# Output steps of a fused attention, GLU and MLP kernel: sums in SBUF or in the output's DRAM rows

## The chip, the core and the metric

The kernel runs on one core of one Trainium2 chip. The metric is the device time of one execution in microseconds (us), here the median of three runs.

## The reference, cut to what matters

Three layers follow one another on 2304 tokens (4 sequences of 576) with a model width of 512. The first is a linear attention over 8 heads, the second a gated MLP (GLU) with d_ff 1536, the third an MLP with d_ff 2048. The change concerns the last product of the third:

```python
def _moe2_ref(x, w_in, w_out) -> np.ndarray:
    h = x @ w_in
    g = h * (1.0 / (1.0 + np.exp(-h)))
    return (g @ w_out).astype(np.float32)
```

The weights are float64 in DRAM. Inputs and outputs of the matmuls are float32, and each operand is split into a high and a low part, so that a product is three matmuls (high x high, high x low, low x high; the list `PASS`).

## The kernel before, in words

Tokens stand in 18 tiles of 128 rows, in five blocks: blocks 0 to 3 of 512 tokens, block 4 of 256. The d_ff of the two MLPs is walked in groups (`groups`). A group of the third layer holds two slices of 128 columns, `fs`, so there are eight groups, from 575.85 us of the span to its end. All 18 tiles pass through each group, so every output element is a sum over eight groups, which is kept in SBUF, in the tiles `ya` (called `o` in `g2_mlp`).

A group does three things. It makes h = SiLU(x @ w_in) for each slice and block: matmuls into a PSUM buffer g (L205; for blocks 0 and 1 the sharing scheme of `quad`, L539; block 4 uses a y buffer), SiLU on ScalarE (ACT, L239 or L562), the high half of h on ACT (L198) and the low half on VectorE (DVE, L199). It makes the output steps (`g2_mlp`, L279): per tile six matmuls into one of four PSUM buffers y (L292), then in the first group a copy to SBUF on ACT (L301), in the seven later groups an add of PSUM to SBUF on DVE (L303). In the last group each finished tile is stored from SyncE's queue (SP, L306); the last tile is done in two halves of 256 columns there. The two tiles of block 4 have rows in two sequences, so that each is stored by two transfers (`out_rows`, L62).

And a group prepares the weights of the next one. SP loads 512 KB of float64 words (L134, L136). DVE shifts and masks them in five operations of 128x512 (L146 to L157), GpSimd (Pool) finishes the float32 value with two integer adds (L160), ACT rounds the high part (L412) and DVE subtracts to get the low part (L416). For the sharing scheme Pool also makes four small sums of the two w_in slices (`sum12`, `sum34`, through `less`, L319), which go through L412 and L416, too.

The order of the work is the order in which the program emits it, and each engine's queue keeps it: the generator `stream` yields after pieces of matmul work, and `WeightQueue.tick` is called at a pace to put the next piece of weight preparation between them. In groups 3 to 7 (the third to the seventh) the emission runs: decode of both w_in slices (`dec`, whose last two steps are L160 on Pool); third-layer matmuls of slice 0 for block 2; step 1 of block 1; high part of the first weight; step 2; its low part and the high part of the second weight; steps 3 and 4; low part, `sum12`; SiLU of slice 0 for block 2; `sum34`; slice 1 for block 2; step 1 of block 0; high part of the first sum; steps 2 to 4; high part of the second sum and decode of the first w_out slice; SiLU of slice 1 for block 2; slice 0 for block 3 with its SiLU; step 1 of block 2; high part of that w_out slice and decode of the second; the other steps of block 2; slice 1 for block 3, both slices for block 4. The steps of blocks 3 and 4 are emitted between the products of the next group's `quad`.

Of the kernel before, what the change touches and what calls it, by code (L numbers as in the profile page):

```python
# [13 lines left out]
AF = mybir.ActivationFunctionType  # L14
ALU = mybir.AluOpType
# [5 lines left out]
def kernel(  # L21
# [14 lines left out]
    nc = tc.nc  # L36
# [8 lines left out]
    TB = 4  # L45
# [16 lines left out]
    def out_rows(i):  # L62
        kind, b, hf, r = tiles[i]
        if kind == "m":
            r0 = b * S + 256 * hf
            return [(0, P, out[r0:r0 + 256, :].rearrange("(p r) d -> p r d", r=2)[:, r, :])]
        return [
            (64 * e, 64 * e + 64, out[(b + e) * S + 512:(b + e) * S + 576, :]) for e in range(2)
        ]
# [29 lines left out]
    def ps_tile(which, shape):  # L99
        p, tag, n = pools[which]  # L100
        return p.tile(shape, F32, tag=tag, name=tag, bufs=n)
# [177 lines left out]
    def g2_mlp(fs, j, hs, first, last, end):  # L279
        wq.need(*[(2, "p", f) for f in fs])  # L280
        nt = blocks[j] // P
        o = ya[j].rearrange("p (t d) -> p t d", t=nt)
        nn = 3 * len(fs)
        cuts = [(t, 0, DM) for t in range(nt)]
        if end:
            cuts[-1:] = [(nt - 1, d, d + DM // 2) for d in (0, DM // 2)]
        for t, d0, d1 in cuts:
            ps = ps_tile("ps_y", [P, DM])[:, d0:d1]
            n = 0
            for f in fs:  # L290
                for a, c in PASS:
                    nc.tensor.matmul(  # L292
                        out=ps,
                        lhsT=hs[f][:, a, t * P:(t + 1) * P],
                        rhs=wt[2, "p", f][:, c, d0:d1],
                        start=(n == 0),
                        stop=(n == nn - 1),
                    )
                    n += 1
            if first:  # L300
                nc.scalar.activation(out=o[:, t, :], in_=ps, func=AF.Copy)  # L301
            else:
                nc.vector.tensor_tensor(out=o[:, t, d0:d1], in0=ps, in1=o[:, t, d0:d1], op=ALU.add)  # L303
            if last:
                for p0, p1, rows in out_rows(j * TB + t):
                    nc.sync.dma_start(out=rows[:, d0:d1], in_=o[p0:p1, t, d0:d1])  # L306
            yield 0.216 * nn

    KH = KC // 2
# [368 lines left out]
    def stream():  # L678
# [25 lines left out]
        for u, (kind, fs) in enumerate(groups):  # L704
# [4 lines left out]
            if std <= u < std + NSTD:  # L709
                out_of = lambda j: g2_mlp(fs, j, hs[j], first, False, False)  # L710
                ys = iter(pend)
                wq.hold = first
                while wait:
                    wait.pop(0)()
                each = [(2, 1), (2, 2), (1, 0), (2, 1)] if first else [(2, 2), (1, 1), (0, 0), (0, 0)]
                for n, k in enumerate(each):
                    if n == 3:
                        ys = chain_of(ys, out_of(0))
                        wq.release(*wq.keys(u - 1)[1])
                    yield from mlp_block(fs[n % 2], n // 2, hs[n // 2], ys, k if n < 3 else (k[0], 9))  # L720
                wq.hold = False
                if first:
                    assert wq.jobs.pop(0)[0] == 1 << 10
                    now, later = token_sums(
                        lambda k: w_tile(1, 7, F32) if k == 2 else wq.slot(("t", k), F32),
                        lambda n: wq.release(("t", 1 - n)),
                    )
                    sums.extend(now)
                if u == std + NSTD - 1:
                    sums.extend(later)  # L730
                yield from g1_mlp(fs[0], 2, hs[2], (), out_of(1))
                yield from g1_mlp(fs[1], 2, hs[2], (), ())
            else:
                yield from quad(u, iter(pend), hs)
# [6 lines left out]
            if kind == 1:  # L741
                f = fs[0]
                out_of = lambda j: g2_glu(fs, j, hs[j], False, done)
                ys = chain_of(out_of(0), out_of(1))
                yield from glu_block(f, 2, hs[2], ys, {"g": 0, "v": 1})
                yield from glu_block(f, 3, hs[3], ys, {"g": 1, "v": 1})
                yield from glu_block(f, 4, hs[4], ys, {"g": 1, "v": 1})
                yield from ys
                pend = chain_of(out_of(2), out_of(3), out_of(4))
                wq.release(*wq.keys(u)[0])  # L750
            else:
                out_of = lambda j, end=False: g2_mlp(fs, j, hs[j], first, last, end)
                if u >= std + NSTD:
                    for n, f in enumerate(fs):
                        yield from g1_mlp(f, 2, hs[2], (), out_of(1 - n))
                if last:
                    yield from g1_mlp(fs[0], 4, hs[4], (), ())
                    yield from g1_mlp(fs[1], 4, hs[4], (), out_of(2))
                    yield from g1_mlp(fs[0], 3, hs[3], (), ())
                    yield from g1_mlp(fs[1], 3, hs[3], out_of(4), ())  # L760
                    yield from out_of(3, True)
                else:
                    yield from g1_mlp(fs[0], 3, hs[3], out_of(2), ())
                    yield from g1_mlp(fs[1], 3, hs[3], (), ())
                    for f in fs:
                        yield from g1_mlp(f, 4, hs[4], (), ())
                    wq.release(*wq.keys(u)[0])
                    pend = chain_of(out_of(3), out_of(4))
# [697 lines left out]
    with tc.manual_schedule():  # L1466
# [21 lines left out]
        def idle(n, deps):  # L1488
            o = Op("warm", "PE", 0.21 * n, warm(n), deps, ["b"])
            o.free.append((o, "b"))  # L1490
            return o
# [4 lines left out]
                out=om, in_=omega.rearrange("m (o d) -> m o d", o=1).to_broadcast([P, 2, D])  # L1496
# [3 lines left out]
        first = idle(5, [])  # L1500
# [74 lines left out]
```

## Time and profile before

| | us |
|---|---|
| median of 3 runs (954.39 to 955.02) | 954.68 |
| the profiled execution, its own time | 954.74 |
| span of the profiled execution, first to last instruction | 952.9 |
| TensorE busy in the span | 942.4 |
| VectorE busy | 705.6 |
| ScalarE busy | 431.9 |
| GpSimd busy | 414.0 |

Busy times count an instruction from its start to its end; issuing DMAs and waiting on semaphores is not counted. PE is TensorE, DVE VectorE, ACT ScalarE, POOL GpSimd, SP SyncE; SPq is the queue of DMA issues on SP. L303 is line 303 of the kernel before. `out<-in` gives the tiles by the program's names: `ya` the sums in SBUF, `y` and `g` PSUM buffers, `m` and `raw` weights in work, `w` and `ws` finished weights and their sums, `h` and `s` activations. A time line has one row for a run of like instructions: start, length, engine, line, and in brackets how long the engine had waited and for whom. In a row by windows the numbers behind the length are the busy times of PE, PEld, DVE, ACT and POOL, each with its count of instructions, then the granted clock of TensorE (1.00 is the full level, 2.4 GHz), the mean share of the 16 DMA engines and GB/s.

### The profile page before, as it was taken

The numbers are of one execution on the slowest core, as the hardware profiler recorded it, in microseconds if no ns is written. First come the engines' busy times: TensorE is split into PE (matmuls) and PEld (weight loads), VectorE is DVE, ScalarE is ACT, GpSimd is POOL, SyncE is SP. The second block draws the span as 40 slices with busy tenths as digits, with TensorE's granted clock in tenths as the row PEclk, the third lists the DMA queues.
The fourth block names the chain that finished last, engine by engine and source line by source line (L and its number), as shares of the span: only waits on it lengthen the run. The fifth ranks groups of instructions, "written<-read, shape, count | busy, mean of one in ns | idle before, by whom it ended". The sixth has DMA issues, their size and how long they took to land.

```text
span 952.9 us, 17029 instructions
## 1 busy us (share of the span) xinstructions
PE 942.4 (99%) x6570; PEld 791.5 (83%) x6570; DVE 705.6 (74%) x1368; ACT 431.9 (45%) x978; POOL 414.0 (43%) x402
## 2 busy tenths in 40 slices
PE   8999999999999999999999999999999999999998
PEld 6888878888888888888888887878888888888887
DVE  6998989648687878779778785887757676767543
ACT  6999977543424323433333355543333333333321
POOL 8888655315445445436335204552424242424200
PEclk9999999999999999999999999999999999999999
DMA  7645443002111121021112100211111111111023
GB/s 181 176 124 157 136 126 101 12 23 74 58 46 45 45 67 45 23 66 52 38 45 67 45 1 27 63 44 45 45 45 45 45 45 45 44 45 45 1 78 122
DMA packets 79489, 60.42 MB, mean 63 GB/s; under 512 B 27312, under 2 KB 73648, under 8 KB 79408
## 3 DMA queue, kind: packets, MB, share of 16 engines
q1 hardware_dynamic: 79136, 59.26, 21.4%
q8 instruction: 52, 0.85, 0.4%
q14 instruction: 29, 0.24, 0.1%
q10 hardware_dynamic: 272, 0.07, 0.0%
HBM read 49.87 MB, written 4.72 MB: 57 GB/s over the span
## 4 chain that ended last, share of the span: by engine, by line
PE 93%; DVE 3%; ACT 1%; DMA 1%; POOL 1%; SPq 1%; issue 0%; DVEq 0%
PE g L205 23%; PE y L292 20%; PE g L539 15%; PE y L259 13%; PE y L205 6%; PE b L1043 3%; PE b L205 2%; PE b L1443 2%; PE kv L1123 2%; PE b L1227 2%; PE b L1016 2%; PE b L1203 1%; PE b L1323 1%; DVE h L199 1%; SPq L1183 0%
## 5 line engine op out<-in xcount | busy, mean ns | idle before, releaser
L160 POOL TENSOR_TENSOR m<-m,raw 128x512 int32<-128x512 int32 x136 | 202.5, 1491 | 322.3 <-issue 209.2
L205 PE MATMUL g<-xs,w 128*128 128x512 f32 x1056 | 256.1, 389 | 0.0
L205 PEld LDWEIGHTS g<-xs,w 128*128 128x128 f32 x1056 | 197.5, 188 | 40.5
L292 PE MATMUL y<-w,h 128*128 128x512 f32 (+1 forms) x870 | 206.9, 388 | 2.3 <-DVE ya L270 1.6
L292 PEld LDWEIGHTS y<-w,h 128*128 128x128 f32 x870 | 162.4, 188 | 36.4 <-issue 1.8
L199 DVE TENSOR_TENSOR h<-s,h 128x512 fp32r<-128x512 f32 (+1 forms) x134 | 107.8, 809 | 77.5 <-ACT h L198 76.4
L259 PE MATMUL y<-h,w 128*128 128x512 f32 (+1 forms) x648 | 155.4, 366 | 0.0
L270 DVE TENSOR_TENSOR ya<-y,ya 128x512 f32<-128x512 f32 (+1 forms) x200 | 122.8, 631 | 20.9 <-PE y L259 20.7
L259 PEld LDWEIGHTS y<-h,w 128*128 128x128 f32 x648 | 113.2, 188 | 20.4 <-DVE h L199 0.5
L303 DVE TENSOR_TENSOR ya<-y,ya 128x512 f32<-128x512 f32 (+1 forms) x127 | 84.4, 680 | 54.4 <-PE y L292 53.9
L198 ACT ACTIVATE h<-s 128x512 fp32r<-128x512 f32 (+1 forms) x134 | 77.1, 585 | 93.7 <-DVE s L644 49.4
L539 PE MATMUL g<-xs,w 128*128 128x512 f32 x360 | 91.7, 390 | 0.0
L412 ACT ACTIVATE w<-m 128x512 fp32r<-128x512 f32 x74 | 46.6, 629 | 84.0 <-POOL m L160 77.4
L416 DVE TENSOR_TENSOR w<-m,w 128x512 fp32r<-128x512 f32 x65 | 66.5, 1024 | 22.2 <-ACT w L412 21.1
L1092 ACT ACTIVATE e<-b,nb 128x128 f32<-128x128 f32 x272 | 75.8, 422 | 7.6 <-PE b L205 2.8
L539 PEld LDWEIGHTS g<-xs,w 128*128 128x128 f32 x360 | 67.1, 188 | 13.9
L539 PE MATMUL g<-w,w 128*128 128x512 f32 x270 | 68.7, 390 | 0.0
L205 PEld LDWEIGHTS y<-xs,w 128*128 128x128 f32 x480 | 60.6, 188 | 2.3
L205 PE MATMUL y<-xs,w 128*128 128x256 f32 x480 | 61.3, 280 | 0.0
L539 PEld LDWEIGHTS g<-w,w 128*128 128x128 f32 x270 | 50.1, 188 | 10.0
L1060 DVE TENSOR_REDUCE small<-b 128x4 f32<-128x512 f32 (+1 forms) x80 | 51.4, 643 | 6.9 <-PE b L1043 3.2
L562 ACT ACTIVATE s<-s 128x512 f32<-128x512 f32 x21 | 13.3, 632 | 77.7 <-DVE s L567 77.7
(120 smaller groups left out, 1159.8 us busy)
## 6 DMA issues: line engine op xcount, KB each, us to landing
raw<-in_moe_w_out_dram SPq DMA_DIRECT2D x28, 512.0 KB, 3.5
raw<-in_moe_w_in_dram SPq DMA_DIRECT2D x16, 512.0 KB, 3.7
raw<-in_moe_w_gate_dram SPq DMA_DIRECT2D x12, 512.0 KB, 3.6
raw<-in_moe_w_val_dram SPq DMA_DIRECT2D x12, 512.0 KB, 3.6
qT<-e SPq DMA_DIRECT2D x72, 64.0 KB, 2.5
x<-in_k_dram SPq DMA_DIRECT2D x16, 256.0 KB, 3.8
x<-in_q_dram SPq DMA_DIRECT2D x16, 256.0 KB, 3.4
va<-in_v_dram SPq DMA_DIRECT2D x32, 128.0 KB, 4.2
```

The lines of the kernel that those rows point to most:

```text
L160: tt(out=mi, in0=mi, in1=(low if step == 5 else high).bitcast(I32), op=ALU.add)
L198: nc.scalar.activation(out=ht[:, 0, :], in_=s, func=AF.Copy)
L199: nc.vector.tensor_tensor(out=ht[:, 1, :], in0=s, in1=ht[:, 0, :].bitcast(F32), op=ALU.subtract)
L205: nc.tensor.matmul(out=ps, lhsT=w[:, a, cc * P:(cc + 1) * P], rhs=xs[j][:, c, cc, :], start=(n == 0), stop=(n == 3 * KC - 1),)
L259: nc.tensor.matmul(out=ps, lhsT=wt[1, "o", f][:, a, d * P:(d + 1) * P], rhs=hs[f][:, c, :], start=(n == 0), stop=(n == nn - 1),)
L270: nc.vector.tensor_tensor(out=y[:, d, :], in0=ps, in1=y[:, d, :], op=ALU.add)
L292: nc.tensor.matmul(out=ps, lhsT=hs[f][:, a, t * P:(t + 1) * P], rhs=wt[2, "p", f][:, c, d0:d1], start=(n == 0), stop=(n == nn - 1),)
L303: nc.vector.tensor_tensor(out=o[:, t, d0:d1], in0=ps, in1=o[:, t, d0:d1], op=ALU.add)
L416: eng.tensor_tensor(out=v[:, 1, :], in0=x, in1=v[:, 0, :].bitcast(F32), op=ALU.subtract)
L539: nc.tensor.matmul(out=ps, lhsT=w[:, a, (c0 + c) * P:(c0 + c + 1) * P], rhs=x(b, c), start=(start and n == 0), stop=(n == 3 * KH - 1), ski ...
L1060: nc.vector.tensor_reduce(out=st.mx.rearrange("p (j e) -> p e j", e=2)[:, e], in_=st.ps[e], axis=AX.X, op=ALU.max)
L1092: nc.scalar.activation(out=st.e[r][:, :, h, :] if blocks4 else st.e[r][:, h, :], in_=src.rearrange("p (a f) -> p a f", a=4) if blocks4 els ...
```

## The change

Every output step is copied from PSUM to its place in SBUF by ACT, whichever group it is in. Right after that a transfer takes it to the output's rows in DRAM: in the first group a plain store from SP's queue, in the later seven a transfer from GpSimd's queue that adds to what stands in the rows. The adds on DVE and the stores of the last group fall away. A group has 18 steps and 20 transfers (two for each tile of block 4); with the halved last tile there are 20 plain stores and 141 adding transfers.

```diff
--- before.py
+++ after.py
@@ -297,13 +297,12 @@
                         stop=(n == nn - 1),
                     )
                     n += 1
-            if first:
-                nc.scalar.activation(out=o[:, t, :], in_=ps, func=AF.Copy)
-            else:
-                nc.vector.tensor_tensor(out=o[:, t, d0:d1], in0=ps, in1=o[:, t, d0:d1], op=ALU.add)
-            if last:
-                for p0, p1, rows in out_rows(j * TB + t):
+            nc.scalar.activation(out=o[:, t, d0:d1], in_=ps, func=AF.Copy)
+            for p0, p1, rows in out_rows(j * TB + t):
+                if first:
                     nc.sync.dma_start(out=rows[:, d0:d1], in_=o[p0:p1, t, d0:d1])
+                else:
+                    nc.gpsimd.dma_start(out=rows[:, d0:d1], in_=o[p0:p1, t, d0:d1], accum_op=ALU.add)
             yield 0.216 * nn
 
     KH = KC // 2
```

## Rows read from the trace of the kernel before

**Rows 1.** The page's parts 1 and 4: engines' busy time, chain that ended last.

```profile
PE 942.4 (99%) x6570; PEld 791.5 (83%) x6570; DVE 705.6 (74%) x1368; ACT 431.9 (45%) x978; POOL 414.0 (43%) x402
...
PE 93%; DVE 3%; ACT 1%; DMA 1%; POOL 1%; SPq 1%; issue 0%; DVEq 0%
```

**Rows 2.** Windows: stretch, length, busy time of the engines, clock, DMA share, GB/s.

```profile
622.00:652.03 30.03, 29.34 (x131) 23.91 (x130) 26.39 (x41) 9.33 (x15) 15.48 (x11) 1.00 0.12 35
702.60:750.35 47.75, 47.75 (x224) 40.01 (x223) 32.55 (x56) 16.52 (x29) 16.83 (x12) 1.00 0.13 40
893.59:949.62 56.03, 56.02 (x265) 46.86 (x263) 24.30 (x38) 14.37 (x26) 0.00 (x0) 1.00 0.22 75
575.85:949.62 373.77, 373.06 (x1741) 312.26 (x1740) 247.62 (x407) 134.17 (x236) 126.84 (x84) 1.00 0.15 48
```

**Rows 3.** The chain in order of time, 622 to 640 us: start, length, what.

```profile
627.65 1.19 DVE ya L303 x2
...
631.83 1.20 DVE ya L303 x2
633.03 0.75 DVE h L199
```

**Rows 4.** Waits of one group, 702.6 to 750.35: in all, times, longest.

```profile
ACT w L412 <- POOL m L160: 11.0, 3, 6.8
...
ACT w L412 <- POOL m L319: 1.2, 1, 1.2
```

**Rows 5.** Groups of instructions, 702.6 to 750.35; the last row from 576 to 952.9.

```profile
L160 POOL TENSOR_TENSOR m<-m,raw 128x512 int32<-128x512 int32 x8 | 13.2, 1650 | 31.4 <-DVE m L157 24.3 <-issue 6.7
L303 DVE TENSOR_TENSOR ya<-y,ya 128x512 f32<-128x512 f32 x18 | 12.0, 683 | 7.0 <-PE y L292 7.0
...
L149 DVE TENSOR_SCALAR raw<-raw 128x512 uint32<-128x512 uint32 x4 | 1.7, 420 | 0.0
...
L319 POOL TENSOR_TENSOR ws<-ws,m 128x256 f32<-128x256 f32 x1 | 1.1, 1090 | 0.1
...
L301 ACT ACTIVATE ya<-y 128x512 f32<-128x512 f32 x18 | 10.7, 597 | 15.3 <-PE y L292 15.2
```

**Rows 6.** The chain in order of time in the same group: start, length, what.

```profile
731.20 5.44 PE y L292 x24
736.64 2.72 PE g L205 x12
739.36 5.44 PE y L292 x24
```

**Rows 7.** Time line of Pool, same group: start, length, what, wait before.

```profile
724.53 7.08 POOL L160 TENSOR_TENSOR m<-m,raw 128x512 int32<-128x512 int32 x4 [24.35 <-DVE m L157]
731.69 0.74 POOL L319 TENSOR_TENSOR ws<-m 128x256 f32<-128x256 f32 x1
...
734.71 0.73 POOL L319 TENSOR_TENSOR m<-m,ws 128x256 f32<-128x256 f32 x1
```

**Rows 8.** Time line of ACT in the same group.

```profile
731.64 0.63 ACT L412 ACTIVATE w<-m 128x512 fp32r<-128x512 f32 x1 [2.35 <-POOL m L160]
...
735.48 0.63 ACT L412 ACTIVATE w<-m 128x512 fp32r<-128x512 f32 x1 [1.22 <-POOL m L319]
736.02 0.58 ACT L239 ACTIVATE s<-g 128x512 f32<-128x512 f32 x1
736.63 0.63 ACT L198 ACTIVATE h<-s 128x512 fp32r<-128x512 f32 x1
```

**Rows 9.** Time line of the end, all engines.

```profile
941.21 8.39 PE L292 MATMUL y<-w,h 128*128 128x512 f32 x42
...
942.04 0.63 ACT L198 ACTIVATE h<-s 128x512 fp32r<-128x512 f32 x1
...
949.64 0.42 DVE L303 TENSOR_TENSOR ya<-y,ya 128x256 f32<-128x256 f32 x1 [0.29 <-PE y L292]
```

**Rows 10.** Loads on the page; the final store's issue and landing; SP's waits, 570 to 952.9.

```profile
raw<-in_moe_w_in_dram SPq DMA_DIRECT2D x16, 512.0 KB, 3.7
...
L306 SPq DMA_DIRECT2D out_dram<-ya x21: 332/333/1127, 916.1 to 950.1; - x21
...
DMA to landing us min/median/max: 1.8/2.1/3.0
...
SPq L306 <- DVE ya L303: 64.8, 16, 40.9
```

## The prediction

> **What bounds the kernel now.** I read the page first. Its span is 952.9 us and TensorE (PE) is busy for 942.4 us of it [rows 1]; the chain that ended last is 93% PE. Only code after 575.85 us changes, so I cut that stage with the view by windows [rows 2]: from 575.85 to 949.62 us PE is busy 373.06 of 373.77 us at the full granted clock. That is 0.71 us of idle time, nearly all of it (30.03 - 29.34) in one place, 622 to 652 us, where PE waits for DVE's low half of h [rows 3]. So nothing can be won in this stage beyond 0.71 us. The question is only what new waits the change makes.
>
> The stage repeats every 47.75 us, one group of two d_ff slices over all five blocks: 18 output steps of six matmuls. In such a group DVE is busy 32.55 us, ACT 16.52 and Pool 16.83 [rows 2]: room on average. But each engine works in program order, and the list of waits [rows 4] shows ACT standing behind Pool for 11.0 us (the weights' high halves, L412, wait for the integer adds of L160). I therefore follow one group in the chain in order of time, which is PE here, and in the time lines of Pool and ACT [rows 6 to 8].
>
> **The change, part by part.**
>
> *Removed.* 127 DVE adds: 18 of 683 ns in a group, 12.0 us [rows 5]. DVE does not bound PE except in the one stall above, on whose chain two pairs of these adds stand [rows 3]. Gain: at most the 0.71 us; I take 0.7. The 21 final stores leave SP, too.
>
> *Added on ACT.* The same steps copied at 597 ns, as the 18 first-group copies show [rows 5]: 10.7 us a group, ACT then 27.2 of 47.75 us. Each copy must free one of four y buffers, and some now stand behind ACT's waits for Pool. Where L412 waits until 731.64 [rows 8], the copies of the third and fourth step of the stretch at 723 us end at about 732.9 and 733.5; PE takes their buffers again at 733.9 and 735.3 (731.20 plus two and three steps of 1.36, [rows 6]). Price nothing, with 1 us of slack.
>
> *First group.* Its 20 plain stores (18 steps, two of them in two halves) go into SP's queue ahead of weight loads: 20 x 0.333 = 6.7 us of issue [rows 10], each waiting for its ACT copy. Behind them wait the raw loads, and for those DVE's decode; a load takes 3.7 us [rows 10] and stands most of a group ahead of its use. I price it at nothing; without that lead it would delay a decode by a step, 1.4 us.
>
> *Added on Pool.* The adding transfers: 20 a group. Let d be Pool's time for issuing one. No row shows it. From below: an SP issue takes 0.33 us [rows 10]. From above: the longest Pool instruction of the group, the L160 add at 1.65 us on average [rows 5]; past 1.55 Pool itself is full (second rival), so this forecast's own range ends there. I take d = 1.1, as the small Pool add of 1.09 us [rows 5] is the nearest thing of Pool's own that is mostly handling. The Trainium skill ("DMA: Bandwidth & Descriptors", Specifications) gives GpSimd's path about 1 us to the first byte and SP's 0.6; by it, as an estimate, the sum below would come to about 971. No run here shows that yet.
>
> Each transfer waits for its ACT copy, and Pool's adds queue behind. Program order on Pool becomes: four L160 adds, transfers 1 to 4, the four sum adds (L319), transfers 5 to 8, two L160 adds, and so on. Today the L160 adds end at 731.61 and the sums follow at once until 735.44 [rows 7]; ACT's last sum copy starts at 735.48, the SiLU that follows at 736.02, its h copy at 736.63 [rows 8]. That h is needed by the output step that starts at 739.36 [rows 6]: its low half at the sixth matmul, about 740.5, so the high half must be ready, with DVE's 0.7, by 739.8. Today it is ready at 737.26 (736.63 + 0.63): slack 2.5 us.
>
> With the change the sums start later by S, the larger of 4d (four issues in a row) and 1.95 + d (the fourth copy ends about 0.63 + 2 x 0.6 us after the adds, with 0.1 for the handing over). For d = 1.1, S = 4.4. Added to it: 0.6 because the decode begins after one more ACT copy and 0.4 for copies crowding between the sum copies. Stall of PE per group: 4.4 + 0.6 + 0.4 - 2.5 = **2.9 us**. Bounds: d = 0.33 gives S = 2.3, a stall of 0.8; d = 1.55 gives S = 6.2, a stall of 4.7. Later in the group, the same reckoning leaves PE unhindered: the weights' second pair is used a group later.
>
> Five groups have this pattern; the group at 622 to 652 us has it in another order, with half the transfers ahead of the sums, and I take half, 1.5 us (0 to 3). Sum: 5 x 2.9 + 1.5 = 16.0.
>
> *The transfers themselves.* 18 x 256 KB = 4.7 MB a group. The last window moved 75 GB/s at a DMA share of 0.22 [rows 2], about 2.9 us of all engines per MB. Taken as read and write at twice that, the transfers need 27 of 47.75 us beside the 0.13 of today: hidden. They would bind at over three times the plain price. That a transfer waits for the one before it I exclude: the stores of before go to one output too, several in flight, and SP's waits have only the adds [rows 10]. The row's earlier transfer is a group old.
>
> *The tail.* Today PE ends at 949.62, the half add takes 0.42, SP issues at once and the store lands 2.1 us later [rows 9, 10]. With the change the last seven copies feed nine transfers, the first copy ending at 943.4, behind ACT's h at 942.67 [rows 9]: at d = 1.1 Pool ends the ninth issue at 943.4 + 9.9 = 953.3, against SP's 950.4: +2.9. One pass through the output rows more: 0 to 2.1, I take 1.0. Tail +3.9; at d = 0.33 it is +0.1 to +2, at d = 1.55 about +8.
>
> **Sum.** The profiled execution took 954.74 us, against a median of 954.68. 954.74 - 0.7 + 16.0 + 3.9 = **973.9**. With the bounds of d: 954.74 - 0.7 + 4 + 0.5 + 1 = 959.5, and 954.74 - 0.7 + 23.5 + 2.5 + 8 = 988.
>
> **Rivals.**
> 1. *Hidden (15%).* The slack of 2.5 us is enough, since DVE is freer and Pool's L160 adds shorten (two-input DVE work beside them falls by 12 us a group), and d is near 0.33. Only the tail grows: 954.74 - 0.7 + 1 to 4 = 955 to 959. For it: low mean load of ACT and Pool. Against: Pool's order, whatever d is, since the fourth copy alone holds the sums back by 1.85 us.
> 2. *Pool, or the DMA engines, become the bound (20%).* Point of decision: 20 d + 16.83 > 47.75, d > 1.55. At d = 2 the group takes 56.8, 9.1 us more, six times, and the tail 12: 954.74 - 0.7 + 54.6 + 12 = 1021. Accumulating at over three times the plain transfer price has the same effect. DVE's decode runs 20 shift and mask operations of 0.42 us a group [rows 5]; if Pool could issue nothing beside them, 8.4 us more would lie on Pool and the point of decision would fall to d = 1.13, close to what I take. That is why this rival has as much as 20%. The Trainium skill ("SBUF — State Buffer", Who interferes with whom) speaks for this: by it, a DVE operation in a two-port mode holds the port that GpSimd needs to write its transfers' descriptors. The rows only hint at it: the L160 adds take 1.65 us on average in this group.
> 3. *Each transfer waits for the former (4%).* 20 x (2.1 + d) + 16.83 = 81 us a group: +33 x 6, about 1155. Against it [rows 10].
> 4. *Not slower (3%).* The DVE chain at 622 to 640 us [rows 3] loses its 2.4 us of adds and PE its stall; the tail stays, because the transfers' issue is no longer than SP's 0.33. Then 954.74 - 0.7 = 954.0. It decides where S stays under 2.5 - 1.0 us, so that every h keeps its slack.
>
> **How the numbers follow.** The forecast gets 58%, its own range 959.5 to 988. The range of 8 in 10 reaches from 957 (half of rival 1) to 1008 (half of rival 2). About 0.2%, 1.9 us, is what a measurement of this kernel can tell from no change. Faster by more would need 1.9 us where PE idles only 0.71: 1%. Same: rival 4 and a third of rival 1, 7%. Slower: 92%.
>
> **What would show it.** DVE's L303 gone, ACT copies of about 0.6 us, Pool instructions or gaps of about 1.1 us per transfer. PE idle of 2 to 4 us once a group, at the output steps after the third g product, released by DVE's or ACT's h (L199, L198); ACT's wait at L412 for Pool's L319 sums grown from about 1 to over 4 us. Wrong: PE as full as before (rival 1), Pool without gaps and the stall elsewhere (rival 2), Pool waiting on DMA (rival 3), or stalls caused by y buffers that ACT frees late.

## The result, and the profile after

| | before | after |
|---|---|---|
| median, us | 954.77 (4 runs, 954.39 to 955.02) | 967.16 (4 runs, 966.57 to 970.18) |
| the profiled execution, its own time | 954.74 | 967.20 |
| its span | 952.9 | 965.4 |

The ratio is 1.0136, with a 95% interval of 1.0115 to 1.0158: 12.4 us slower. The prediction was slower, 973.9 us, so its direction held, the measured time lies inside both of its ranges, and the forecast loss of 19.2 us was too large by 6.8.

The page of after, its parts 1 and 4 and a row of its DMA issues (KB each, median us to landing), beside [rows 1]:

```profile
PE 945.7 (98%) x6570; PEld 790.7 (82%) x6570; DVE 643.2 (67%) x1241; ACT 499.4 (52%) x1105; POOL 533.0 (55%) x543
...
PE 75%; POOL 8%; ACT 7%; DVE 5%; issue 2%; DMA 2%; SPq 1%; POOLq 0%; DVEq 0%; ACTq 0%
...
out_dram<-ya POOLq DMA_DIRECT2D x111, 256.0 KB, 6.1
```

127 DVE instructions are gone, ACT has 127 more, and Pool has 141 more, the adding transfers, which the page counts as busy. On average no engine came nearer to full than PE. But PE's share of the chain that ended last fell from 93% to 75%. A part of that lies ahead of the stage (ACT's L1091, 2%); within it, Pool and ACT now end waits of PE, as the rows below show.

Where the 12.5 us of span went is read from the chain of waits in order of time. Each group of the last six begins with a product of the sharing scheme (L539, in after L538, 549 and the like). The starts of three of them in after, at 704.52, 753.27 and 803.37, against 702.60, 750.35 and 798.10 before:

```profile
704.52 1.39 PE g L538 x6
...
753.27 1.39 PE g L538 x6
...
803.37 1.40 PE g L538 x6
```

Taking all six starts (655.71, 704.52, 753.27, 803.37, 852.19, 900.98 against 654.86 to 893.59) and the span's end splits each profiled execution into four pieces. The same split serves for all the kernels below (the chain of the doubled kernel leaves out the first start, so that one is from PE's time line). Numbers are us beyond the kernel before; the first column is code that no kernel here changes (up to PE's first product at 570.58 in before), so it is scatter between executions, up to 1.7 us.

| kernel | ahead of the stage | to the first start | five groups | last group and end |
|---|---|---|---|---|
| after | +0.2 | +0.6 | **+6.5** | **+5.1** |
| copies alone | +1.6 | +2.9 | 0.0 | 0.0 |
| plain transfers from Pool | +1.5 | +1.3 | +1.4 | +1.4 |
| DVE adds, plain transfers from Pool | +1.7 | +0.1 | +3.9 | +1.5 |
| block 1's transfers behind the sums | +0.6 | +0.7 | +5.9 | +6.1 |
| twice as many transfers | +0.8 | +2.1 | +34.4 | +11.5 |
| transfers of blocks 0 and 1 moved on | 0.0 | +1.3 | 0.0 | +6.4 |
| the same, end as before | -0.3 | +1.3 | 0.0 | +0.1 |
| as after, end as before | -1.7 | +3.5 | +6.1 | +0.2 |

So after loses in two places that have little to do with each other, the five steady groups and the end.

**The steady group.** The chain in order of time inside the group that begins at 704.52 (start, length, what):

```profile
726.22 2.76 POOL m L160
...
733.30 3.54 POOL out_dram L305 x4
736.83 0.93 POOL ws L318
...
739.14 1.56 ACT ya L300 x3
740.70 0.52 ACT w L411
741.22 0.50 ACT s L239
...
741.74 0.64 ACT h L198
...
742.42 5.30 PE y L292 x21
```

In [rows 7] the four sums follow the integer adds after 0.08 us. Now four transfers stand between them, 3.54 us. Then the chain runs as the prediction drew it: Pool's sums, ACT's copy of the last sum (behind three output copies), the SiLU (L239), the high half of h (L198), the output step. PE's time line has the idle time in its brackets, with the engine that ended it:

```profile
741.12 0.84 PE L292 MATMUL y<-w,h 128*128 128x512 f32 x3
742.42 5.30 PE L292 MATMUL y<-w,h 128*128 128x512 f32 x21 [0.47 <-ACT h L198]
```

The row shows 0.47 us, and the whole group is 48.75 - 47.75 = 1.00 us longer. The list of waits of the same group (704.52 to 753.27; us in all, times, longest) has the weight loads of the same step waiting for the low half of h, and ACT behind Pool, where [rows 4] had 11.0 and 1.2:

```profile
ACT w L411 <- POOL m L160: 7.9, 3, 3.4
...
ACT w L411 <- POOL ws L318: 2.0, 1, 2.0
...
PE y L292 <- ACT h L198: 0.5, 1, 0.5
PEld y L292 <- DVE h L199: 0.4, 1, 0.4
```

So of the signs that the prediction named, ACT's wait for the sums grew less than it said (2.0, not over 4), and the releasers of PE are the two named. The stall is first the high half of h, then the low half. Four of the five groups lost 1.0 to 1.1 us, and one 2.4.

**The end.** The chain in order of time, and the end by windows, in the columns of [rows 2]:

```profile
955.14 1.12 POOL out_dram L305
...
957.03 1.21 POOL out_dram L305
958.25 0.89 POOLq L1569
```

```profile
948.00:965.40 17.40, 8.99 (x46) 7.50 (x44) 0.76 (x2) 4.99 (x9) 7.85 (x9) 0.84 0.65 97
```

PE ends at about 957.0 and Pool has issued its last transfer at 958.24. The span ends 7.2 us later, where before it ended 2.5 us after the last store's issue. What fills those 7 us is the view of DMA for the same stretch (40 slices, the digit is the busy share of the 16 engines in tenths; then the queue's packets, MB and share):

```profile
DMA  9300000000978999998999999999999992000000
...
q0 software_dynamic: 1109, 1.68, 64.6%
```

From the eleventh slice, 952.4 us, on to about 962 the DMA engines are nearly full, with no more than these last output rows.

**The price of an adding transfer.** The view of line L305 in after (duration of Pool's record, min/median/max in ns; landing in us), and DMA from 640 to 940 us:

```profile
L305 POOL DMA_DIRECT2D out_dram<-ya x141: 816/1042/2109, 630.7 to 957.7; - x141
...
DMA to landing us min/median/max: 3.0/5.8/9.6
```

```profile
q0 software_dynamic: 16352, 29.43, 64.2%
```

64.2% of 300 us for 29.43 MB is 6.5 us of all 16 engines per MB.

### The profile page after: what moved, and what is told of

Read it like the earlier page. It is cut to its first block, busy times and chain, and to the rows that moved or that the text cites. A ratio compares the mean times of both kernels' runs of the same rounds, so it can differ in the third digit from the quotient of the medians.

```text
span 965.4 us, 17434 instructions
## 1 busy us (share of the span) xinstructions
PE 945.7 (98%) x6570; PEld 790.7 (82%) x6570; DVE 643.2 (67%) x1241; ACT 499.4 (52%) x1105; POOL 533.0 (55%) x543
## 4 chain that ended last, share of the span: by engine, by line
PE 75%; POOL 8%; ACT 7%; DVE 5%; issue 2%; DMA 2%; SPq 1%; POOLq 0%; DVEq 0%; ACTq 0%
PE g L205 19%; PE g L538 14%; PE y L259 13%; PE y L292 13%; PE y L205 6%; POOL m L160 3%; POOL out_dram L305 3%; PE b L1042 2%; PE b L1442 2%; PE b L205 2%; ACT e L1091 2%; ACT ya L300 1%; ACT h L198 1%; PE b L1015 1%; PE b L1226 1%
## 5 line engine op out<-in xcount | busy, mean ns | idle before, releaser
L160 POOL TENSOR_TENSOR m<-m,raw 128x512 int32<-128x512 int32 x136 | 209.4, 1542 | 182.8 <-DVE m L157 59.9
L292 PE MATMUL y<-w,h 128*128 128x512 f32 (+1 forms) x870 | 209.9, 389 | 6.6 <-DVE h L199 2.6
L199 DVE TENSOR_TENSOR h<-s,h 128x512 fp32r<-128x512 f32 (+1 forms) x134 | 116.1, 869 | 117.1 <-ACT h L198 115.5
L305 POOL DMA_DIRECT2D out_dram<-ya x141 | 126.5, 1136 | 89.4 <-ACT ya L300 80.9
L270 DVE TENSOR_TENSOR ya<-y,ya 128x512 f32<-128x512 f32 (+1 forms) x200 | 122.7, 630 | 20.9 <-PE y L259 20.7
L198 ACT ACTIVATE h<-s 128x512 fp32r<-128x512 f32 (+1 forms) x134 | 77.7, 585 | 89.4 <-DVE s L643 49.4
L300 ACT ACTIVATE ya<-y 128x512 f32<-128x512 f32 (+1 forms) x145 | 83.0, 590 | 71.5 <-PE y L292 71.1
L538 PE MATMUL g<-xs,w 128*128 128x512 f32 x360 | 91.7, 390 | 0.0
L1091 ACT ACTIVATE e<-b,nb 128x128 f32<-128x128 f32 x272 | 76.1, 425 | 8.2 <-PE b L205 3.0
L538 PEld LDWEIGHTS g<-xs,w 128*128 128x128 f32 x360 | 67.1, 188 | 13.9
L538 PE MATMUL g<-w,w 128*128 128x512 f32 x270 | 68.8, 390 | 0.0
L538 PEld LDWEIGHTS g<-w,w 128*128 128x128 f32 x270 | 50.1, 188 | 10.0
```

Of the source, the lines that this page charges most:

```text
L160: tt(out=mi, in0=mi, in1=(low if step == 5 else high).bitcast(I32), op=ALU.add)
L198: nc.scalar.activation(out=ht[:, 0, :], in_=s, func=AF.Copy)
L199: nc.vector.tensor_tensor(out=ht[:, 1, :], in0=s, in1=ht[:, 0, :].bitcast(F32), op=ALU.subtract)
L270: nc.vector.tensor_tensor(out=y[:, d, :], in0=ps, in1=y[:, d, :], op=ALU.add)
L292: nc.tensor.matmul(out=ps, lhsT=hs[f][:, a, t * P:(t + 1) * P], rhs=wt[2, "p", f][:, c, d0:d1], start=(n == 0), stop=(n == nn - 1),)
L300: nc.scalar.activation(out=o[:, t, d0:d1], in_=ps, func=AF.Copy)
```

## The experiments

All edits are against the changed kernel. In the theory on record, transfers that stand in Pool's queue ahead of the four sums make them late; its rivals were ACT's copies and the transfers' traffic.

### Copies alone

```diff
             nc.scalar.activation(out=o[:, t, d0:d1], in_=ps, func=AF.Copy)
-            for p0, p1, rows in out_rows(j * TB + t):
-                if first:
+            if last:
+                for p0, p1, rows in out_rows(j * TB + t):
                     nc.sync.dma_start(out=rows[:, d0:d1], in_=o[p0:p1, t, d0:d1])
-                else:
-                    nc.gpsimd.dma_start(out=rows[:, d0:d1], in_=o[p0:p1, t, d0:d1], accum_op=ALU.add)
```

> Every step is copied by ACT, but no transfer leaves before the last group, whose stores go out on SP's queue: the additions over the groups are left out, and so are all GpSimd transfers. Theory 1 (the four sum adds on GpSimd stand behind four transfers, so h comes late): no transfers, no stall, 954.0 to 955.0 us, group period 47.75 us. Rival A (ACT's 127 extra copies delay its SiLU and high halves): the period stays near 48.8 us, 960 to 962 us. Rival B (the adding transfers' traffic): 954 to 955 us, like theory 1.

Measured: 954.48 us (952.78 to 959.14), ratio 0.999 (0.9977 to 1.0003). In the stretch 655 to 890, in the columns of [rows 2], PE has no gap:

```profile
655.00:890.00 235.00, 235.00 (x1095) 196.89 (x1094) 104.16 (x192) 129.12 (x234) 81.80 (x61) 1.00 0.15 45
```

ACT does the same copies as in after, 129 us of 235, and nothing is lost here. In these groups copying instead of adding costs nothing, and gains nothing. The profiled execution (959.14) was 2.9 us longer in the group at 622 to 652 us; the median lies 4.7 below it, as much as that and its 1.6 ahead of the stage, so most executions seem not to have them.

### Transfers from Pool that don't add

```diff
-                    nc.gpsimd.dma_start(out=rows[:, d0:d1], in_=o[p0:p1, t, d0:d1], accum_op=ALU.add)
+                    nc.gpsimd.dma_start(out=rows[:, d0:d1], in_=o[p0:p1, t, d0:d1])
```

> The transfers of the later groups stay on GpSimd's queue but only store: the addition over the groups is left out. Issue and order on GpSimd are unchanged. Theory 1: the period stays near 48.8 us in groups 3 to 7, and only the end shortens, by the 4 to 5 us that the adding transfers take longer to land: 962 to 963.5 us. Rival A: the same. Rival B (traffic of reading and adding): period back to 47.75 us, 955 to 957 us. DMA share falls from about 0.77 to about 0.45 if an adding transfer costs twice a plain one.

Measured: 958.76 us (956.92 to 961.77), ratio 1.0039 (1.0026 to 1.0052): between the two expectations. A group takes 48.02 us, a stall of 0.27. The view of the line and the DMA of 640 to 940 us say why, beside the rows of after:

```profile
L305 POOL DMA_DIRECT2D out_dram<-ya x141: 534/542/777, 633.3 to 954.4; - x141
...
DMA to landing us min/median/max: 2.2/2.7/5.9
```

```profile
q0 software_dynamic: 9453, 30.40, 28.3%
```

A plain issue holds Pool for 0.54 us, an adding one 0.89 (four in 3.54 us). So the order on Pool alone was tested here at a lower dose: in Pool's time line the integer adds end at 734.48 and the sums start 2.5 us later, not 3.5. And a plain transfer costs the DMA engines 2.8 us per MB (28.3% of 300 us for 30.40 MB) against 6.5: adding is 2.3 times as dear.

### DVE adds as before, Pool only carries

```diff
-            nc.scalar.activation(out=o[:, t, d0:d1], in_=ps, func=AF.Copy)
+            if first:
+                nc.scalar.activation(out=o[:, t, :], in_=ps, func=AF.Copy)
+            else:
+                nc.vector.tensor_tensor(out=o[:, t, d0:d1], in0=ps, in1=o[:, t, d0:d1], op=ALU.add)
             for p0, p1, rows in out_rows(j * TB + t):
-                if first:
-                    nc.sync.dma_start(out=rows[:, d0:d1], in_=o[p0:p1, t, d0:d1])
-                else:
-                    nc.gpsimd.dma_start(out=rows[:, d0:d1], in_=o[p0:p1, t, d0:d1], accum_op=ALU.add)
+                if not first:
+                    nc.gpsimd.dma_start(out=rows[:, d0:d1], in_=o[p0:p1, t, d0:d1])
```

> The sums stay in SBUF by DVE's adds as before the change, ACT copies nothing, and GpSimd's queue stores the running sums after each step of the later groups (the last store holds the full sum). Theory 1: the sums on GpSimd stand behind the same four transfers, the period is 48.4 to 49.5 us, the end is short: 959 to 964 us. Rival A (ACT's copies): period 47.75 us, 955 to 957 us. Rival B: 955 to 957 us.

Measured: 961.16 us (959.27 to 961.76), ratio 1.0058 (1.0038 to 1.0077). A group takes 48.51 us. Pool's time line, and PE's:

```profile
734.04 2.18 POOL L306 DMA_DIRECT2D out_dram<-ya  x4
736.23 0.99 POOL L319 TENSOR_TENSOR ws<-m 128x256 f32<-128x256 f32 x1
```

```profile
743.52 4.60 PE L292 MATMUL y<-w,h 128*128 128x512 f32 x19 [0.47 <-DVE h L199]
```

With none of the copies in the later groups on ACT, the sums are still late, by 2.2 us, and PE still stalls, now for the low half of h, since DVE has its adds back. The stall comes with the transfers on Pool, not with the copies.

### Block 1's transfers behind the sums

```diff
-            for p0, p1, rows in out_rows(j * TB + t):
...
+            def send(t=t, d0=d0, d1=d1):
...
+            if j == 1 and not first:
+                held.append(send)
+            else:
+                if held:
+                    held.pop(0)()
+                send()
```

> Everything as in the changed kernel, but the four transfers of block 1 are issued one by one with the next block's transfers, so that they stand behind the four sum adds in GpSimd's queue and not ahead of them. Theory 1: the sums follow the weight adds at once, the stall at the third stretch of output steps goes, period 47.75 to 47.9 us, five groups give back 6.5 us: 960 to 961.5 us; the end is as long as in the changed kernel. Rivals A and B: nothing changes, 966 to 968 us.

Measured: 968.13 us (967.69 to 969.89), ratio 1.0137 (1.0118 to 1.0157). A miss: no faster than after. Pool's time line shows the edit at work, and what it did next; DVE's and PE's show who stalls:

```profile
733.97 0.74 POOL L329 TENSOR_TENSOR ws<-m 128x256 f32<-128x256 f32 x1
...
737.22 7.47 POOL L309 DMA_DIRECT2D out_dram<-ya  x8
741.92 5.65 POOL L160 TENSOR_TENSOR m<-m,raw 128x512 int32<-128x512 int32 x2
```

```profile
741.44 2.32 DVE L199 TENSOR_TENSOR h<-s,h 128x512 fp32r<-128x512 f32 x1 [1.28 <-ACT h L198]
```

```profile
743.81 4.60 PE L294 MATMUL y<-w,h 128*128 128x512 f32 x19 [0.87 <-DVE h L199]
```

The sums now start 0.1 us after the integer adds, as before the change. But eight transfers follow in one row, 737.22 to 744.68, ahead of the next weight's integer adds, and among them DVE's low half of h takes 2.32 us, where the median of that line in after is 0.69. PE waits for that instead. So "the sums are late" was true and not enough: whatever Pool does in this part of the group lies on the path to h, in one way or the other. The theory became: the transfers of blocks 0 and 1, anywhere between the decode and the last h, cost PE time; moved past it they cost none.

### Twice as many transfers

```diff
-                    nc.gpsimd.dma_start(out=rows[:, d0:d1], in_=o[p0:p1, t, d0:d1], accum_op=ALU.add)
+                    dm = (d0 + d1) // 2
+                    for a, b in ((d0, dm), (dm, d1)):
+                        nc.gpsimd.dma_start(out=rows[:, a:b], in_=o[p0:p1, t, a:b], accum_op=ALU.add)
```

> The changed kernel with each adding transfer cut into two halves of 256 columns: the same bytes, twice the issues on GpSimd. Theory 2 (GpSimd works in order, so every microsecond of issuing ahead of its sum adds and weight adds makes h late): at 0.7 to 0.9 us for an issue the sums start 2 to 3.5 us later, and GpSimd's 40 issues and 17 us of adds come to 45 to 53 us of a group of 48.8: period 51 to 54 us, 978 to 998 us. Rival B (the traffic's bytes): 966 to 970 us.

Measured: 1004.55 us (1002.3 to 1005.27), ratio 1.0513 (1.05 to 1.0527). The same bytes in twice the issues: the direction as expected, the size beyond it. A group takes 54.6 us, 6.9 more than before, and Pool is busy for 215.86 us of the 235 from 655 to 890. Of the 6.9, PE's time line gives 4.12 as waiting; the windows give the rest:

```profile
754.11 7.45 PE L292 MATMUL y<-w,h 128*128 128x512 f32 x21 [4.12 <-ACT h L198]
```

```profile
746.00:752.00 6.00, 3.99 (x18) 2.98 (x16) 1.03 (x1) 1.70 (x4) 5.92 (x9) 1.00 1.02 138
752.00:758.00 6.00, 3.89 (x9) 3.07 (x10) 5.87 (x8) 3.74 (x7) 6.00 (x9) 0.53 0.86 100
758.00:764.00 6.00, 6.00 (x25) 4.86 (x25) 5.35 (x8) 2.01 (x4) 5.92 (x7) 0.90 0.71 95
```

After the gap the granted clock is near the lower of its two levels (0.53 of 2.4 GHz), and the 21 matmuls that follow take 7.45 us, against 5.30 for the 21 of after that follow its gap of 0.47 with no clock lost (1.00). So a gap of 4 us cost 2 us more behind it.

### The end as before, first try

```diff
+    BY_DMA = (0, 1, 2)
...
+            if first or j in BY_DMA:
...
+                nc.vector.tensor_tensor(out=o[:, t, d0:d1], in0=ps, in1=o[:, t, d0:d1], op=ALU.add)
```

> Blocks 3 and 4, whose steps end the kernel, are summed in SBUF by DVE and stored from SP's queue as before the change; blocks 0 to 2 as in the changed kernel. Theory 2: the groups keep their stall (48.5 to 48.9 us, the transfers of blocks 3 and 4 were issued while GpSimd was idle), the end takes 59.3 to 59.8 us again from the last group's start instead of 64.6: 961 to 963 us. If the transfers of blocks 3 and 4 do take part in the stall, the period falls to 47.8 to 48.2: 956 to 959 us.

Measured: 955.03 us (954.26 to 957.51), ratio 0.9998 (0.9989 to 1.0007), and it says nothing about the end: the name `BY_DMA` is assigned again further down the kernel (`range(18, 36)`), before these steps run, so no block was treated as in after and the kernel did the work of before. It is a repeat of that, no more.

### Transfers of blocks 0 and 1 moved past the last h

```diff
-            for p0, p1, rows in out_rows(j * TB + t):
...
+            def send(t=t, d0=d0, d1=d1):
...
+            if j < 2 and not first and not last:
+                held.append(send)
+            else:
+                if held:
+                    held.pop(0)()
+                send()
```

> All transfers kept, but those of blocks 1 and 0 are held back and issued one by one with the steps of blocks 2, 3 and 4, so that neither the four sum adds nor the first w_out slice's weight adds on GpSimd stand behind transfers; the last group issues at once as in the changed kernel. Theory 2 (GpSimd's order does the harm in two ways: late sums, and weight adds pushed to where they hold up DVE's low half of h): both go, period 47.75 to 48.0 us, 959.5 to 961.5 us. Theory 1 (late sums alone) was not borne out by moving only block 1's transfers; if the traffic is the cause (rival B), the period stays at 48.8 to 48.9 us: 966 to 968.5 us.

Measured: 962.37 us (960.18 to 965.83), ratio 1.0079 (1.0062 to 1.0095), a little above what was expected. The five groups take 47.75 us each again. The chain, the window beside that of after, and DVE's time line:

```profile
703.83 1.39 PE g L549 x6
...
751.57 1.39 PE g L549 x6
```

```profile
655.00:890.00 235.00, 235.00 (x1088) 196.54 (x1087) 105.93 (x191) 128.97 (x233) 167.66 (x159) 1.00 0.73 145
```

```profile
655.00:890.00 235.00, 231.46 (x1060) 190.70 (x1058) 111.38 (x182) 123.20 (x226) 161.37 (x155) 1.00 0.78 139
```

```profile
740.20 0.69 DVE L199 TENSOR_TENSOR h<-s,h 128x512 fp32r<-128x512 f32 x1 [1.33 <-ACT h L198]
```

As many adding transfers as in after, as many bytes, Pool as busy (167.66 us against 161.37), DMA share 0.73: and PE never waits. With the chain of after this settles where the stall comes from: the transfers' place in Pool's order (and so in time), not their number, their bytes or ACT's copies. It does not show what lengthened DVE's low half in the fourth experiment. The end is still 6.4 us longer than before, and the group at 622 to 652 us 1.3.

### The same, with the end as before

```diff
+            by_dma = j < 3
+            if first or by_dma:
+                nc.scalar.activation(out=o[:, t, d0:d1], in_=ps, func=AF.Copy)
+            else:
+                nc.vector.tensor_tensor(out=o[:, t, d0:d1], in0=ps, in1=o[:, t, d0:d1], op=ALU.add)
...
+                    elif first if by_dma else last:
+                        nc.sync.dma_start(out=rows[:, d0:d1], in_=o[p0:p1, t, d0:d1])
```

> Both repairs together: transfers of blocks 1 and 0 held back, blocks 3 and 4 summed on DVE and stored from SP as before the change. Theory 2 with the end priced apart: 954.5 to 956 us, no different from the kernel before. Rival B: the period stays above 48.3 us: 958 us or more.

Measured: 957.12 us (954.06 to 958.77), ratio 1.0019 (1.0007 to 1.003), 1.1 above the expected range. Blocks 3 and 4, whose steps come last, are summed on DVE and stored by SP, and the end is within 0.1 us of before. The two losses add up: 6.5 and 5.1 are both gone. What is left in the profiled execution (955.81) is 1.3 us in the group at 622 to 652 us. It is the best version with adding transfers, and does not beat the kernel before.

### The end as before, the rest as changed

```diff
+    ROWS_J = (0, 1, 2)
...
+            if first or j in ROWS_J:
+                nc.scalar.activation(out=o[:, t, d0:d1], in_=ps, func=AF.Copy)
+            else:
+                nc.vector.tensor_tensor(out=o[:, t, d0:d1], in0=ps, in1=o[:, t, d0:d1], op=ALU.add)
```

> The run before this under nearly the same name did not carry its edit, this one does: blocks 3 and 4, whose steps end the kernel, are summed in SBUF by DVE and stored from SP's queue as before the change; blocks 0 to 2 as in the changed kernel. Theory 2 (GpSimd's order): the groups keep their stall, as the transfers of blocks 3 and 4 were issued while GpSimd had nothing else to do, period 48.5 to 48.9 us; the end takes 59.3 to 59.8 us from the last group's start instead of 64.6: 960.5 to 963 us. Were the transfers of blocks 3 and 4, or the traffic as a whole, part of the stall, the period would fall to 47.75 to 48.2 us: 955 to 958 us.

Measured: 964.62 us (962.66 to 966.84), ratio 1.0105 (1.0081 to 1.013), above what was expected. The two places behave as the theory has them: the five groups lose 6.1 us (after: 6.5), the end 0.2 (after: 5.1). The excess is in the group at 622 to 652 us, 3.5 against 0.6.

## Why the prediction was right, and where its sizes were off

**The bound.** As read: PE was full, so the change could win only 0.7 us, and everything turned on new waits. The copies alone (no change that can be measured) show that the room on ACT was real and that DVE's adds were worth nothing. The 0.7 us taken as a gain were not won: in every kernel but the doubled one the wait at 632 us stayed or grew (last paragraphs of this section).

**ACT's copies and the first group's stores at nothing.** Right: copies alone lose nothing in the five groups, and behind the stores PE is busy for 46.00 of 46.00 us in after, from 576 to 622. Up to the first start after loses 0.6 us, with the group at 622 to 652 us in it; the forecast was -0.7 + 1.5 = 0.8. That is luck: the 0.7 was not won, and no wait behind the sums shows there; the 0.6 are DVE's low half of h, which takes 2.02 us in after (from 632.63) and 0.82 in before.

**The stall, 2.9 us a group, measured 1.0 to 1.1 in four of five.** The mechanism and its place were right: four transfers, then the sums, then ACT's sum copy, SiLU and h, and PE idle released by ACT's L198. The terms, each as a shift within the group against before:

- S, the sums' later start: forecast 4.4 from d = 1.1. Measured 3.5: d is 0.89 in a row, and 4d = 3.54 less the 0.08 that was there before. In the second experiment, with d = 0.54, the other arm, 1.95 + 0.54 = 2.5, is the larger, and the sums did start 2.5 later.
- The decode's later start: forecast +0.6. Measured -0.2 (the integer adds end 28.83 us into the group, before 29.01).
- The sums themselves, not in the forecast: they end 3.15 us after they may start (736.83 to 739.98), before it was 3.75 (731.69 to 735.44, [rows 7]). -0.6.
- The copies between the sums and ACT's last sum copy: forecast +0.4, measured +0.6.

Together h is late by 3.2 us (741.74 - 704.52 = 37.22 against 736.63 - 702.60 = 34.03), forecast 5.4. Less the slack of 2.5 that leaves 0.7 against a measured 1.0 to 1.1; so the slack was a few tenths too generous: what waits for the low half is the weight load of the sixth matmul (the PEld row above), and weight loads start 0.2 us ahead of their matmuls there (740.89 against 741.12). DVE's own order, which the prediction did not follow, was nearly as late: in after its decode ended at 742.28, the high half at 742.37. The mis-sized step is "d = 1.1" together with "0.6 because the decode begins after one more ACT copy". Over the five groups that makes 6.5 us instead of 14.5. The Trainium skill's estimate ("DMA: Bandwidth & Descriptors", Specifications; 1 us for GpSimd's path) gave 971; it states a latency, and Pool's hold on the queue was measured at 0.54 us for a plain and 0.89 for an adding transfer.

The one group with 2.4 us is the miss with "Later in the group, the same reckoning leaves PE unhindered". There the low half of h took 2.02 us, as in the fourth experiment. This row is from the chain in order of time of after:

```profile
791.15 2.02 DVE h L199
```

The Trainium skill ("SBUF — State Buffer", Who interferes with whom) says that a DVE operation with two inputs in SBUF and a GpSimd operation that reads SBUF shut each other out for a whole instruction. The trace agrees in kind: 2.0 and 2.3 us for an operation of 0.69, with Pool at its transfers and adds. Transfers are not needed for it: in before, where Pool issues none, a low half of h takes 1.79 us beside the second of two integer adds (the two run from 739.18 to 742.53).

```profile
741.29 1.79 DVE L199 TENSOR_TENSOR h<-s,h 128x512 fp32r<-128x512 f32 x1
```

Which of Pool's instructions holds it in after and in the fourth experiment the rows do not tell, since the records of transfers and adds overlap; in the row of the seventh experiment, 0.69 us stood beside an integer add.

**The end, +3.9 us, measured +5.1.** Near, but by luck, through two errors of opposite sign. Pool's issue was forecast to end 2.9 us later behind PE; it came 0.4 later (1.2 us after PE's end, before 0.8), as nine issues took 7.2 us and not 9.9, and kept up with PE. "One pass through the output rows more: 0 to 2.1, I take 1.0" measured 4.7 (7.2 against 2.5): the bound was too low, because it priced landing by a plain store. The kernel with plain transfers loses 1.4 us at the end, so some 3.7 of the 5.1 are the adding itself.

**The transfers hidden.** Right in the steady groups: DMA share 0.78 in 655 to 890 us, forecast 27 of 47.75 + 0.13 = 0.70; adding costs 2.3 times the plain transfer, taken as twice. "They would bind at over three times" was not reached, except in the end, where no matmul covers them.

**The rivals.** Hidden (1) fell by its own counter-argument, Pool's order; what it would have looked like is the steady group of the seventh experiment. Pool as the bound (2) needed d over 1.55, or over 1.13 if DVE's decode held up Pool's issues. It didn't. Pool's time line of after has four issues beside a decode, 0.1 us each longer than the four in 3.54:

```profile
739.91 3.91 POOL L305 DMA_DIRECT2D out_dram<-ya  x4
```

Doubling the issues came near the state that the rival describes. One transfer waiting for the former (3) is excluded by four issues in 3.54 us while each lands 5.8 us later. Not slower (4) did not happen; with the order and the end mended it nearly did (957.12).

**What stays open: the group at 622 to 652 us.** It lost between 0.1 and 3.5 us from kernel to kernel. In all of them but the doubled one this lies at one output step, the one that begins at 631.84 in before. From there to its sixth matmul it takes 1.99 us in before, 2.68 in after, 3.25 to 3.29 in the copies alone, the plain transfers and the two kernels with moved transfers, and 3.90 in the last. PE's time line in before, and with plain transfers:

```profile
633.83 4.60 PE L292 MATMUL y<-w,h 128*128 128x512 f32 x19 [0.69 <-DVE h L199]
```

```profile
635.23 0.73 PE L292 MATMUL y<-w,h 128*128 128x512 f32 x2 [1.07 <-ACT h L198]
636.57 4.62 PE L292 MATMUL y<-w,h 128*128 128x512 f32 x19 [0.61 <-DVE h L199]
```

The copies alone have the same waits (1.07 and 0.65) and no transfer on Pool, so Pool's issues are not needed for them. ACT's h stands there behind ACT's wait for the first two integer adds, and these took longer. Pool's time line in before, and with plain transfers:

```profile
627.78 2.76 POOL L160 TENSOR_TENSOR m<-m,raw 128x512 int32<-128x512 int32 x2 [2.36 <-issue]
```

```profile
629.26 4.11 POOL L160 TENSOR_TENSOR m<-m,raw 128x512 int32<-128x512 int32 x2 [2.36 <-ACT ya L300]
```

With DVE's own adds gone, its two decodes run there without a break, beside these integer adds. In the five kernels in which PE waits for ACT's h, the two adds take 4.1 us and DVE's shift and mask operations 0.42 each; in after, as in the fourth and fifth experiment, the adds take 2.8 us and two of DVE's operations 1.53 each. So one of the two engines lost time beside the other, now this one, now that. No edit explains which, and what sets it stays open. In the copies alone and in the last kernel the 19 matmuls behind the wait take 6.2 us instead of 4.6, at a granted clock of 0.66 (636 to 640 us) and 0.74 (632 to 636): that is the other 1.6 of their 2.9 and 3.5 us. The 1.3, 1.3 and 3.5 us are more than what the seventh, the eighth and the last experiment lie above their expectations.

## What to carry to other kernels

A transfer issued from a computing engine's queue is an instruction of that engine with a price (here 0.5 to 0.9 us) and a wait for its data, and what stands behind it in program order pays for both; room on average says nothing about that. Before moving DMA issues to such a queue, list what is emitted behind each and how much slack its last consumer has, and look again after moving them, as the wait may only change its releaser. An accumulation in DRAM that is hidden in the steady state still shows at the end, where its last transfers land with nothing to cover them: let the last blocks go the old way. And work taken off an engine moves the rest of its order: without the adds, DVE's decodes came to run beside Pool's integer adds without a break, and PE lost up to 3.5 us there.

## What was not expected of the hardware

- Adding costs in three places at once: issue 0.89 us in a row on Pool instead of 0.54, 6.5 us of all DMA engines per MB instead of 2.8, landing 5.8 us instead of 2.7 (medians of 141 transfers each, in two kernels that differ in `accum_op` alone).
- Records of issues on Pool overlap what follows them: in the fourth experiment the integer adds' record begins at 741.92, while transfers ahead of them end at 744.68. The ends, 0.9 us apart, give the price of one; the median record of 1.04 us in after is too long for that.
- A gap of 4.12 us in PE was followed by matmuls at a granted clock of 0.53; gaps of 0.46 and 1.31 us in the longest group of after were not (1.00). For gaps of that size it went either way: 1.07 and 0.65 us, two matmuls apart, were followed by 0.66 in the copies alone, and 1.07 and 0.61 with plain transfers by 1.00.
- Where DVE's shift and mask operations met Pool's integer adds (at 626 to 633 us), either an operation of 0.42 us took 1.53, or two adds took 4.1 us instead of 2.8.
